# MLP products of an attention-and-MLP kernel: three float32r products of split operands in place of bilinear schemes, from the third unit on

## The chip, the cores and the metric

The kernel runs on one core of a Trainium2 chip. A core has five engines that matter here, each with a queue of its own that it works off in order: PE multiplies matrices, DVE and ACT work elementwise (ACT also evaluates functions), POOL is a slower elementwise engine, and SP issues DMAs. They wait for each other through semaphores. The metric is the device time of one execution in microseconds (us); the kernel before takes 545.12 us (median of three runs, 545.11 to 545.23).

## The reference

Two blocks follow each other. The first is a gated linear attention with a state per head, the second an MLP with an ELU between its two matrices:

```python
f = 1.0 / (1.0 + np.exp(-f_logit))                       # (4, 8, 768, 48)
for t in range(S):
    state = f[:, :, t, :, None] * state + np.einsum('bhd,bhe->bhde', k[:, :, t], v[:, :, t])
    y[:, :, t] = np.einsum('bhd,bhde->bhe', q[:, :, t], state)
x = y.transpose(0, 2, 1, 3).reshape(4 * 768, 8 * 48)     # 3072 tokens of 384
h = x @ w_in                                             # w_in (384, 2048), float64 on input
g = np.where(h > 0.0, h, np.exp(np.minimum(h, 0.0)) - 1.0)
out = g @ w_out                                          # w_out (2048, 384)
```

## The kernel before

The 3072 tokens are worked off as 12 units of 256 tokens, three to each of the four sequences. For a unit the attention is computed first, which leaves the unit's 256 rows of x, transposed (384 x 256), and then the MLP. The MLP of one unit and the attention of the next are interleaved: the program is written out in positions T, `plan` holds for each position the pieces of attention and other side work (`at_step`), and the main loop at the end of `fast` puts the MLP's matmuls between them. What is recorded in this order is each engine's queue order; no scheduler moves anything.

Attention of a unit, with the functions that do it: `load` fetches f, k, q and v; `gates` (ACT) and `grow` (a running product on DVE) make the decays, `fall` their reciprocals on DVE; `scale` multiplies them into k and q on POOL; `move` copies two of the decay rows' pieces to the fourth head pair with a DMA on SP's queue; `transposed` turns k on PE; `advance` makes the four chunks' state updates on PE and `step` adds them up on DVE; `scores` multiplies k and q on PE and `mask` cuts off the upper triangle on DVE; `outputs` and `carried` multiply by v and the state on PE, and ACT copies the result to x. Tiles of q, k and f are there twice, so that two units can be under way.

The weights come in as float64. `fetch`, `split`, `lower` and `merge` bring them in and make float32 of them during units 0 and 1; later `reread` and `check` read them again and look for values out of range, which is no part of the result but of a flag that chooses between this program and a general one.

In units 0 and 1 the up product (x by `w_in`) is plain: `up` takes two 128-column blocks of the hidden layer at a time, 3 x 2 matmuls of 256 columns. Unit 0's down product and two pairs of unit 1's are plain too (`down`, matmuls of 384 or 192 columns); the other pairs of unit 1 and all that follow use a 2 x 2 scheme with seven products for eight, whose sums of weights `combine` makes beforehand and whose sums of activations `elu` puts on POOL. From unit 2 on the up product uses a scheme with 20 products for 24: `phase` multiplies 128 x 128 blocks of weights, or sums of such (`w_sums`), by blocks of x or their sums (`blend`), and `joins` puts the results together on DVE, in the order that the tables `PHASES`, `JOIN3`, `MID`, `JOIN4` and `LAST` set. `exped` and `elu` are the ELU: two ACT operations and one DVE operation on 512 columns. All matmuls are float32. There are 20 positions T per unit from unit 2 on, and the tables `D2` to `D6`, `A2` and `A3` say at which of them attention's pieces stand: the third entry of `D5` and `D6`, -5, is that of the third decay and of `move`, the second entry of `A3`, 9, that of `advance` and `scores`.

Of the kernel before, what the change touches and what calls it, by code (L numbers as in the profile page):

```python
# [11 lines left out]
U16 = mybir.dt.uint16  # L12
AF = mybir.ActivationFunctionType
# [343 lines left out]
def fast(ctx: ExitStack, tc: tile.TileContext, q, k, v, f_logit, w_in, w_out, out, flag, outer):  # L357
# [7 lines left out]

# [26 lines left out]
    DH = DM // 2  # L392
    DIRECT = 1
    PLAIN_UP = 2
    NQ = NP // 2
    PLAIN = 2
    LAG = 2
    AHEAD = 7
# [4 lines left out]
    MORE = 3  # L403
    RR = 2
    HOLD = 2
    A1 = (2, 8, 10, 11)
    D2 = (16, 18, 20, 22)
    A2 = (23, 25, 25, 26, 27, 28)
    D3 = (-9, -6, -3, 1)
    D4 = (-9, -5, -1, 1)  # L410
    D5 = (-15, -9, -5, 1)
    D6 = (-19, -15, -5, 1)
    A3 = (3, 9, 12, 13)
    BL = 16
    BL2 = 29
    CB = 18
    LIMIT = 2.0**80

    X_SUMS = (
        ((12, 13), (1, 2), (0, 0)), ((10, 11), (2, 2), (3, 4)), ((9, 14), (1, 4), (5, 10)),  # L420
        ((8, 15), (0, 13), (9, 10)), ((1, 2), (3, 14), (1, 5)), ((6, 7), (4, 11), (8, 9)),
    )
    W_SUMS = (
# [4 lines left out]
    )  # L428
    EARLY = 10
    PHASES = (  # L430
# [5 lines left out]
    )  # L436
    SEED = (1, 3)
    JOIN3 = (
        (ALU.add, (4, 11), (4, 11), 1, (1, 2)), (ALU.add, (0, 12), (4, 9), 1, (0, 3)), (ALU.subtract, 4, 6, 1, 1, True),
    )  # L440
    MID = (ALU.add, (1, 5), (1, 5), None, (9, 11)), (ALU.subtract, (8, 9), (5, 5), None, (8, 12))
    JOIN4 = (ALU.add, (3, 6), (2, 11), 0, (0, 2)), (ALU.subtract, 2, 3, 0, 3)
    LAST = ((ALU.add, (3, 7), (3, 10), None, (4, 7)),)
    PLACES = ((0, ((0, 1), (1, 1), (1, 0), (0, 0))), (6, ((1, 0), (0, 0), (1, 1), (0, 1))))
    USUAL = ((0, 0), (0, 1), (1, 0), (1, 1))
# [7 lines left out]
    sb = ctx.enter_context(tc.tile_pool(name="sb", bufs=2))  # L453
    ps = ctx.enter_context(tc.tile_pool(name="ps", bufs=1, space=bass.MemoryType.PSUM))

    NB = 2

    qkf = [
        {n: cst.tile([128, HP, 2, U] if n == "f" else [128, HP, U], FP32, name=f"{n}{i}") for n in "fqk"}
        for i in range(NB)  # L460
    ]
    src = {"q": q, "k": k, "f": f_logit}
    vs = [cst.tile([128, NW, PAD + DM + PAD], FP32, name=f"v{i}") for i in range(NB)]
    kn = cst.tile([128, HP, NW, 128], FP32, name="kn")
    ats, xts, sts, pys = {}, {}, {}, {}

    def load(u, names="fkqv"):
        b, s0 = u // UPB, (u % UPB) * U
        for n in names.replace("v", ""):
            to = qkf[u % NB][n][MAIN]  # L470
            frm = src[n][b, :, :, s0 : s0 + U].rearrange("(p r) d s -> (r d) p s", r=2)
            if n == "f":
                to, frm = to[:, 0:NKT, 0], frm[:, 0:NKT]
            nc.sync.dma_start(out=to, in_=frm)
            for r in range(2 if n == "f" or n == "k" and u > 1 else 0):
                gap = qkf[u % NB][n][GAP[r] : GAP[r] + PAD, 0:NKT]
                nc.sync.dma_start(
                    out=gap[:, :, 0] if n == "f" else gap,
                    in_=src[n][b, 2 * NKT + r, :, s0 : s0 + U].rearrange("(i j) s -> i j s", i=PAD),
                )  # L480
# [912 lines left out]
```

## Time and profile before

| | |
|---|---|
| median of three runs | 545.12 us |
| span of the profiled execution | 544.3 us |
| instructions in it | 15606 |
| granted PE clock, mean | 0.998 |
| PE / DVE / ACT / POOL busy in the span | 528.5 / 407.5 / 314.5 / 338.4 us |
| units 0 and 1's MLP | 33.7 to 119.6 us |
| units 2 to 11's MLP | 119.6 to 539.1 us |

The profile names groups of instructions by line, engine, operation, output and inputs. "PE" rows are matmuls, "PEld" the loads of their weights. A float32 matmul leaves two records. Busy times are sums over the records of an engine, so that a share near 100% says that the engine hardly waited; "idle before" in a group's row is how long its engine stood still before these instructions, and what released it. The chain of waits is followed back from the last instruction: where a stretch of it belongs to PE, PE was what everything waited for.

### The profile page before, as it was taken

What the parts mean: (1) busy time and instruction counts of PE and PEld (TensorE: products, weight loads), DVE (VectorE), ACT (ScalarE), POOL (GpSimd) and SP (SyncE); (2) the same over time, 40 slices, a digit from 0 to 9 for tenths busy, and PEclk for the clock granted to TensorE, in tenths of its full rate; (3) what the DMA queues carried; (4) which work ended last, traced back from release to release, by engine and by line L of the source; (5) the groups of instructions that cost most, each with busy time, mean ns of one, the idle gap of its engine ahead of it and who ended that gap; (6) DMA issues with size and microseconds to landing.
All of it is one profiled execution on the core that took longest, in us unless ns stands there. A gap on an engine that the chain in (4) does not pass through costs nothing.

```text
span 544.3 us, 15606 instructions
## 1 busy us (share of the span) xinstructions
PE 528.5 (97%) x6294; PEld 492.8 (91%) x6294; DVE 407.5 (75%) x718; ACT 314.5 (58%) x644; POOL 338.4 (62%) x560
## 2 busy tenths in 40 slices
PE   6889999999999999999999999999999999999996
PEld 3477778899999999899999999999999999999995
DVE  8988988875978886687687687677777865644663
ACT  3289775136565567567567566566675565574441
POOL 6600337678898298298298288378478567454452
PEclk9999999999999999999999999999999999999999
DMA  8998971024052271271261252153243212110001
GB/s 211 256 272 233 282 191 47 2 51 104 30 126 80 57 200 30 61 202 32 61 183 52 60 148 86 60 140 94 60 133 102 61 29 83 50 50 1 29 3 36
DMA packets 39475, 54.30 MB, mean 100 GB/s; under 512 B 4032, under 2 KB 29216, under 8 KB 39392
## 3 DMA queue, kind: packets, MB, share of 16 engines
q1 hardware_dynamic: 38592, 52.61, 36.1%
q8 instruction: 51, 0.84, 0.7%
q10 hardware_dynamic: 800, 0.59, 0.4%
q14 instruction: 32, 0.26, 0.2%
HBM read 45.02 MB, written 4.72 MB: 91 GB/s over the span
## 4 chain that ended last, share of the span: by engine, by line
PE 89%; DMA 6%; DVE 2%; POOL 1%; issue 0%; ACT 0%; SPq 0%; ACTq 0%; DVEq 0%; POOLq 0%
PE psM L1063 37%; PE psH L965 33%; PE psH L989 6%; DMA area<-in_moe_w_in_dram 4%; PE psM L1025 3%; PE psY L804 2%; PE psY L828 2%; PE psU_a L789 2%; PE psS L766 2%; PE psT L726 1%; DMA f<-f 1%; DMA k<-in_k_dram 1%; DVE vals L955 1%; POOL k L678 0%; DVE gg L999 0%
## 5 line engine op out<-in xcount | busy, mean ns | idle before, releaser
L1012 POOL TENSOR_TENSOR sums<-gg 128x128 f32<-128x128 f32 x172 | 101.8, 611 | 124.1 <-DVE gg L999 119.1
L971 ACT COPY vals<-psH 128x512 f32<-128x512 f32 (+1 forms) x120 | 65.4, 545 | 122.2 <-PE psH L965 122.0
L965 PE MATMUL psH<-xt,wi 128*128 128x128 f32 x880 | 131.4, 276 | 0.1
L955 DVE TENSOR_TENSOR vals<-vals,psH 128x256 f32<-128x256 f32 (+1 forms) x160 | 61.8, 386 | 85.0 <-PE psH L965 46.3
L965 PE MATMUL psH<-xt,area 128*128 128x128 f32 x720 | 118.0, 277 | 0.5 <-DVE vals L955 0.4
L965 PEld LDWEIGHTS psH<-xt,wi 128*128 128x128 f32 x880 | 115.2, 192 | 0.7 <-DVE gg L999 0.3
L1063 PE MATMUL psM<-area,sums 128*128 128x192 f32 x516 | 103.3, 326 | 0.0
L965 PEld LDWEIGHTS psH<-xt,area 128*128 128x128 f32 x720 | 100.8, 191 | 2.0 <-PE psS L766 0.7
L1063 PEld LDWEIGHTS psM<-area,sums 128*128 128x128 f32 x516 | 85.9, 190 | 0.0
L1063 PE MATMUL psM<-wo,gg 128*128 128x192 f32 x376 | 76.7, 329 | 0.0
L999 DVE SCALAR_TENSOR_TENSOR gg<-gg,vals 128x512 f32<-128x512 f32 x80 | 64.1, 837 | 9.4 <-ACT gg L980 9.4
L955 DVE TENSOR_TENSOR vals<-vals 128x256 f32<-128x256 f32 x120 | 64.2, 549 | 2.0
L688 DVE RECIPROCAL f<-f 128x256 f32<-128x256 f32 x36 | 62.8, 1748 | 1.1
L1063 PEld LDWEIGHTS psM<-wo,gg 128*128 128x128 f32 x376 | 61.1, 190 | 1.8 <-DVE at L774 1.6
L980 ACT ACTIVATE gg<-gg 128x512 f32<-128x512 f32 x96 | 60.5, 631 | 3.1
L979 ACT ACTIVATE gg<-vals 128x512 f32<-128x512 f32 x80 | 49.5, 619 | 17.5 <-DVE vals L955 17.3
L678 POOL TENSOR_TENSOR k<-k,f 128x256 f32<-128x256 f32 x48 | 36.0, 752 | 32.0 <-DVE f L683 23.4
L678 POOL TENSOR_TENSOR q<-q,f 128x256 f32<-128x256 f32 x48 | 39.6, 826 | 18.8 <-DMA f<-f 14.6
L945 POOL TENSOR_TENSOR xt<-xt 128x256 f32<-128x256 f32 x57 | 48.6, 868 | 3.2 <-DVE xt L945 1.8
L1012 POOL TENSOR_TENSOR sums<-sums,gg 128x128 f32<-128x128 f32 x86 | 47.5, 552 | 0.2
L989 PE MATMUL psH<-xt,wi 128*128 128x256 f32 x192 | 44.8, 383 | 2.3 <-DVE xt L885 1.7
L1012 POOL TENSOR_TENSOR sums<-gg,sums 128x128 f32<-128x128 f32 x86 | 40.5, 471 | 6.6
(113 smaller groups left out, 741.8 us busy)
## 6 DMA issues: line engine op xcount, KB each, us to landing
area<-in_moe_w_out_dram SPq DMA_DIRECT2D x8, 768.0 KB, 10.6
again<-in_moe_w_in_dram SPq DMA_DIRECT2D x16, 384.0 KB, 4.5
again<-in_moe_w_out_dram SPq DMA_DIRECT2D x16, 384.0 KB, 3.6
k<-in_k_dram SPq DMA_DIRECT2D x12, 384.0 KB, 4.2
q<-in_q_dram SPq DMA_DIRECT2D x12, 384.0 KB, 5.4
v<-in_v_dram SPq DMA_DIRECT2D x12, 384.0 KB, 5.7
area<-in_moe_w_in_dram SPq DMA_DIRECT2D x8, 576.0 KB, 8.7
out_dram<-o SPq DMA_DIRECT2D x42, 96.0 KB, 1.7
```

The costliest lines, as they stand in the source:

```text
L678: e.tensor_tensor(out=t[n][:, p], in0=t[n][:, p], in1=t["f"][:, p, "kq".index(n)], op=ALU.mult)
L688: nc.vector.reciprocal(f[:, p, 1], f[:, p, 0])
L945: e.tensor_tensor(out=pick(x, to), in0=pick(x, a), in1=pick(x, b), op=ALU.subtract)
L955: nc.vector.tensor_tensor(out=pick(v, to), in0=x, in1=y, op=op)
L965: nc.tensor.matmul(bank[:, slot], lhsT=w_block(q, w), rhs=xts[m][:, x], start=(i < 2 and t == 0), stop=True, skip_group_check=True,)
L971: nc.scalar.copy(v[:, at : at + size], bank[:, frm : frm + size])
L979: nc.scalar.activation(g[:], h, AF.Relu, scale=-1.0)
L980: nc.scalar.activation(g[:], g[:], AF.Exp, scale=-1.0)
L989: nc.tensor.matmul(ph[:, i], lhsT=wi[j][:, kt, i * 128 : (i + 1) * 128], rhs=xts[m][:, 2 * kt : 2 * kt + 2].rearrange("n t f -> n (t f)"), ...
L999: nc.vector.scalar_tensor_tensor(out=g[:], in0=g[:], scalar=-1.0, in1=phs.pop(P), op0=ALU.add, op1=ALU.max)
L1012: nc.gpsimd.tensor_tensor(out=s[:, i], in0=x, in1=y, op=op)
L1063: nc.tensor.matmul(pm[bank][:, half * DH : (half + 1) * DH], lhsT=x, rhs=y, start=first, stop=(j == NP - 1), skip_group_check=True,)
```

## The change

The bilinear schemes, with their tables, weight sums and joins, are gone. Units 0 and 1 are plain in both products. From unit 2 on each float32 operand a is written as three float32r tiles of at most 12 significant bits (h, l and a sum or difference of them, scaled by powers of two), and a product of two float32 matrices is three matmuls that add up in two PSUM banks:

- `pieces` splits a weight item of 768 columns once: one ACT operation, one DVE operation, and a third part on DVE or on POOL (two operations there). Eleven of the 16 items are split during unit 1, five during unit 2. The parts lie where the float64 and float32 forms lay.
- `factor` splits x of a unit, `cut` the activations g, both through `parted`: ACT makes h, DVE l, POOL the difference. There is one tile of split x for all units, and two slots of split g.
- `top` does the up product of one 128-column block in nine matmuls of 256 columns, `joined` puts its two banks together (a copy on ACT, one operation on DVE), `curve` and `bent` are the ELU, `fold` does the down product in six matmuls of 384 columns, four positions (`BEHIND`) after `top`. `finish` puts the down product's two banks together at the end of a unit.

A unit has 16 positions now. f, k, q and v have one tile each from unit 2 on, so `attention(u)` runs from position -4 to 11 of the unit before. `check` takes 24 pieces of 512 columns in place of 32 of 384.

```diff
-    PHASES = (
-        (0, 1, 0, 3, ((1, 8, 16), (0, 9, 13), (2, 14, 12))),
...
+    E = 2.0**-12
+    CUT = 1.0 - 2.0**-13
...
+    def pieces(n, last):
+        tops[n] = sb.tile([128, 2, 2 * DM], F32R, tag=f"p{n}", name=f"top{n}")
+        h, l = tops[n][:, 0], tops[n][:, 1]
+        nc.scalar.activation(h, full[n][:], AF.Copy, scale=CUT / E)
+        nc.vector.scalar_tensor_tensor(
+            out=l, in0=full[n][:], scalar=1.0 / E, in1=h.bitcast(FP32), op0=ALU.mult, op1=ALU.subtract
+        )
+        rests[n] = sb.tile([128, 2 * DM], F32R, tag=f"r{n}", name=f"rest{n}")
+        d = rests[n][:]
+        if last is nc.vector:
...
+        nc.gpsimd.tensor_scalar(out=d, in0=h.bitcast(FP32), scalar1=-E, scalar2=None, op0=ALU.mult)
+        nc.gpsimd.tensor_tensor(out=d, in0=d.bitcast(FP32), in1=l.bitcast(FP32), op=ALU.add)
...
-    def attention(u, first, then):
+    def attention(u):
+        t = (u - 1) * NFT
...
+            at_step(t - 4, lambda: load(u))
+        at_step(t - 2, lambda: gates(u, bias=0))
...
+        at_step(t - 1, one, *(lambda p=p: (grow(u, p), scale(u, ("k", p, gp))) for p in range(2)))
+        at_step(t + 1, lambda: grow(u, 2), lambda: watch(u), lambda: scale(u, ("k", 2, gp)), lambda: move(u, 0, nc.sync))
+        at_step(t + 2, lambda: transposed(u, 0, "a0"), lambda: transposed(u, 1, "a1"))
+        at_step(t + 3, lambda: fall(u, 0), lambda: scale(u, ("k", NKT, gp), ("q", 0, gp)))
+        at_step(t + 4, lambda: advance(u))
+        at_step(t + 5, lambda: fall(u, 1), lambda: scale(u, ("q", 1, gp)))
+        at_step(t + 6, *(lambda c=c: step(u, c) for c in range(NC - 1)))
+        at_step(t + 7, lambda: fall(u, 2), lambda: scale(u, ("q", 2, gp)), lambda: move(u, 1, nc.sync))
+        at_step(t + 8, lambda: step(u, NC - 1), lambda: scale(u, ("q", NKT, gp)))
+        at_step(t + 9, lambda: kept.append(scores(u)), lambda: mask(u, kept[0]))
+        at_step(t + 10, lambda: outputs(u))
+        at_step(t + 11, lambda: carried(u))
...
+    def parted(x, to, halves):
+        h, l, d = to
+        nc.scalar.activation(h, x, AF.Copy, scale=CUT * E)
+        nc.vector.scalar_tensor_tensor(
+            out=l, in0=h.bitcast(FP32), scalar=-1.0 / E, in1=x, op0=ALU.mult, op1=ALU.add
+        )
...
+            nc.gpsimd.tensor_tensor(out=d[:, c], in0=h[:, c].bitcast(FP32), in1=l[:, c].bitcast(FP32), op=ALU.subtract)
...
+        for kt in kts:
+            for i in range(3):
+                nc.tensor.matmul(
+                    ph[:, i == 2], lhsT=ws[i][:, kt, s % 2 * 128 : s % 2 * 128 + 128], rhs=x[:, i, kt],
...
+    def joined(T):
...
+        nc.scalar.copy(to, ph[:, 1])
+        nc.vector.scalar_tensor_tensor(out=to, in0=ph[:, 0], scalar=1.0 + E, in1=to, op0=ALU.mult, op1=ALU.add)
...
+        for t in range(NW):
+            for n in range(3):
+                nc.tensor.matmul(
+                    pms[m][2 * t + (n == 2)][:], lhsT=g[:, P % 2, n, i * U + t * 128 : i * U + (t + 1) * 128],
+                    rhs=ws[n][:, i], start=(s == 0 and n != 1), stop=(s == NFT - 1), skip_group_check=True,
...
+    for T in range(begin, end + BEHIND):
+        u, s = divmod(T, NFT)
...
+            top(T)
...
+                bent(P - 1)
...
+            joined(T)
+        if T % 2 == 0 and begin < T <= end:
+            cut(P - 1)
+        if T % 2 and T < end:
+            curve(P)
         for f in plan.pop(T, ()):
             f()
...
+            fold(T - BEHIND)
```

On DVE in a unit in the middle, before: `vals` are the joins of the up product (L955), `gg` the ELU (L999), `f` the decays: a scan (L683) and a reciprocal (L688).

```order
L707 SCALAR_TENSOR_TENSOR fine<-f_71,fine 128x3
L683 SCALAR_TENSOR_TENSOR f_68<-f_68 128x256
L688 RECIPROCAL f_68<-f_68 128x256
L955 TENSOR_TENSOR vals_128<-vals_128,psH_0_1_3164 128x2x128 x2
L955 TENSOR_TENSOR vals_128<-psH_0_1_3164,vals_128 128x128
L999 SCALAR_TENSOR_TENSOR gg_6_3181<-gg_6_3181,vals_129 128x512
L999 SCALAR_TENSOR_TENSOR gg_7_3184<-gg_7_3184,vals_129 128x512
```

On DVE in the changed program, positions 7 to 9 of a unit: `v` is written by `joined` (L972), `g` with 128x512 by `bent` (L982) and by the split's subtraction (L943), `state` by `step`, `at` by `mask`, and L641 is `fall`.

```order
L972 SCALAR_TENSOR_TENSOR v_3742<-psH_3758,v_3742 128x256
L641 RECIPROCAL f_74<-f_74 128x256
L982 SCALAR_TENSOR_TENSOR g_3770<-g_3770,v_3742 128x512
L972 SCALAR_TENSOR_TENSOR v_3794<-psH_3783,v_3794 128x256
L943 SCALAR_TENSOR_TENSOR g_1260<-g_1260,g_3770 128x512
L691 TENSOR_TENSOR state<-psU_a_3661,state 128x4x48
L696 TENSOR_TENSOR state<-state,f_74 128x4x48
L972 SCALAR_TENSOR_TENSOR v_3794<-psH_3814,v_3794 128x256
L718 TENSOR_TENSOR at_3863<-psS_0_3829,twice 128x512
```

The reciprocal stood between joins of a program that had 20 positions per unit; it now stands between `joined` and `bent` of the running pair, and the state operation L696, which reads the decay row that `move` copies, stands ahead of the next `joined`.

On PE in the changed program, the same place: `psM` rows are `fold` (L1001), `psH` rows `top` (L960), and the first two of `scores`' 32 matmuls (L709) follow.

```order
L1001 MATMUL psM_0_3698<-top_1074,g_1260 128x384 x2
L1001 MATMUL psM_1_3699<-rest_1077,g_1260 128x384
L1001 MATMUL psM_2_3700<-top_1074,g_1260 128x384 x2
L1001 MATMUL psM_3_3701<-rest_1077,g_1260 128x384
L960 MATMUL psH_3814<-x_1173,top_1027 128x256 x2
L960 MATMUL psH_3814<-x_1173,rest_1030 128x256
L709 MATMUL psS_0_3829<-q_75,k_76 64x64
L709 MATMUL psS_1_3830<-q_75,k_76 64x64
```

Before, the scores stood directly behind the state updates `psU`; now five positions lie between them, and the scores stand two positions behind the last reciprocal.

More of the change, by code (lines that the diff above doesn't have):

```diff
@@ L12 @@
 U16 = mybir.dt.uint16
+F32R = mybir.dt.float32r
 AF = mybir.ActivationFunctionType
@@ L584, in fast, with shaped @@
-    order = [divmod(i, NP) for i in range(NU * NP)]
-    needs = sorted(
-        (2 * P + out_ * (2 * LAG + 1), j, out_) for P, (m, j) in enumerate(order) if m == 0 for out_ in range(2)
-    )
+    raws, full, tops, rests = {}, {}, {}, {}
+    needs = sorted((2 * j + out_ * (2 * LAG + 1), j, out_) for j in range(NP) for out_ in range(2))
     parts = [need[1:] for need in needs]
+    item = {part: n for n, part in enumerate(parts)}
+    def shaped(n, x):
+        return x.rearrange("p (k f) -> p k f", k=2 if parts[n][1] else NKT)
@@ new lines, in fast, with finish, store @@
+    left = []
+    def finish(m, sums):
+        o = outer.tile([128, NW, DM], FP32, tag="o", name=f"o{m}", bufs=1)
+        for t, (a, b) in enumerate(sums):
+            nc.scalar.copy(o[:, t], b[:])
+            if a is not None:
+                nc.vector.scalar_tensor_tensor(
+                    out=o[:, t], in0=a[:], scalar=1.0 + E, in1=o[:, t], op0=ALU.mult, op1=ALU.add
+                )
+        def store(*queues):
+            for t in range(NW):
+                queues[t].dma_start(out=out[m * U + t * 128 : m * U + (t + 1) * 128, :], in_=o[:, t])
+        if m == NU - 1:
+            left.append(store)
+        else:
+            store(nc.sync, nc.sync)
@@ new lines, in down @@
+    def down(P):
+        m, j = divmod(P, NP)
+        if j == 0:
+            banks = (("m1", "m2"), ("m3", "m0"))[m]
+            pms[m] = [ps.tile([128, DM], FP32, tag=banks[t], name=f"psM{m}_{t}") for t in range(NW)]
+        g = gs.pop(P)
+        for i in range(2):
+            for t in range(NW):
+                nc.tensor.matmul(
+                    pms[m][t][:], lhsT=g[:, i * U + t * 128 : i * U + (t + 1) * 128], rhs=weight(j, 1)[:, i],
+                    start=(j == 0 and i == 0), stop=(j == NP - 1 and i == 1),
+                )
+        if j == NP - 1:
+            finish(m, [(None, b) for b in pms.pop(m)])
@@ new lines, in parted, with top @@
+        n = x.shape[1] // halves
+        for i in range(halves):
+            c = slice(i * n, (i + 1) * n)
+            nc.gpsimd.tensor_tensor(out=d[:, c], in0=h[:, c].bitcast(FP32), in1=l[:, c].bitcast(FP32), op=ALU.subtract)
+    def top(T, kts=range(NKT)):
+        s = T % NFT
+        if T not in phs:
+            phs[T] = ps.tile([128, 2, U], FP32, tag=f"h{T % 2}", name=f"psH{T}")
+        ph, x = phs[T], exact["x"]
+        ws = three(s // 2, 0)
+        for kt in kts:
+            for i in range(3):
+                nc.tensor.matmul(
+                    ph[:, i == 2], lhsT=ws[i][:, kt, s % 2 * 128 : s % 2 * 128 + 128], rhs=x[:, i, kt],
+                    start=(kt == i == 0), stop=(kt == NKT - 1 and i > 0), skip_group_check=True,
+                )
@@ new lines, in bent, with cut, fold @@
+    def bent(P):
+        g = gs[P][:]
+        nc.vector.scalar_tensor_tensor(
+            out=g, in0=g, scalar=-1.0, in1=phs.pop(-P), op0=ALU.add, op1=ALU.max
+        )
+        del hs[P]
+    def cut(P):
+        if "g" not in exact:
+            exact["g"] = sb.tile([128, 2, 3, 2 * U], F32R, tag="wide", name="g3")
+        parted(gs.pop(P)[:], [exact["g"][:, P % 2, i] for i in range(3)], 2)
+    def fold(T):
+        m, s = divmod(T, NFT)
+        if s == 0:
+            pms[m] = [ps.tile([128, DM], FP32, tag=f"m{i}", name=f"psM{m}_{i}") for i in range(2 * NW)]
+        ws, g = three(s // 2, 1), exact["g"]
+        P, i = divmod(T, 2)
+        for t in range(NW):
+            for n in range(3):
+                nc.tensor.matmul(
+                    pms[m][2 * t + (n == 2)][:], lhsT=g[:, P % 2, n, i * U + t * 128 : i * U + (t + 1) * 128],
+                    rhs=ws[n][:, i], start=(s == 0 and n != 1), stop=(s == NFT - 1), skip_group_check=True,
+                )
+        if s == NFT - 1:
+            p = pms.pop(m)
+            finish(m, [(p[2 * t], p[2 * t + 1]) for t in range(NW)])
```

607 lines of the change are left out of this document (185 added, 422 removed), and 8 rows, old and new, of tables (PHASES, W_SUMS).

## The prediction

> **What bounds the kernel now.** I read the page's shares first, then the busy time by stage, then the chain that ended last.
>
> ```profile
> PE 528.5 (97%) x6294; PEld 492.8 (91%) x6294; DVE 407.5 (75%) x718; ACT 314.5 (58%) x644; POOL 338.4 (62%) x560
> ...
> 33.70:119.60 85.90, 85.09 (x884) 68.64 (x883) 72.51 (x106) 52.83 (x66) 37.85 (x52) 1.00 0.55 143
> 119.60:537.50 417.90, 417.01 (x5054) 407.84 (x5053) 303.79 (x570) 249.30 (x559) 281.82 (x464) 1.00 0.29 80
> ...
> 240.69 1.63 PE psM L1063 x10
> 282.38 1.63 PE psM L1063 x10
> ```
>
> The second row is units 0 and 1, the third units 2 to 11: PE is busy in 417.01 of 417.90 us, DVE in 303.79. The two chain rows are the same piece of work one unit apart, 41.7 us. So a unit costs what its matmuls cost, and everything on DVE, ACT and POOL is hidden. The prices of the matmuls are in the chain too, as stretches in which PE waits for nobody:
>
> ```profile
> 73.42 2.59 PE psH L989 x12
> 76.01 2.58 PE psM L1025 x8
> 254.94 2.23 PE psH L965 x20
> 257.17 2.28 PE psM L1063 x14
> ```
>
> A float32 product leaves two records. One record takes 215.8 ns at 256 columns (2.59/12), 322.5 at 384 (2.58/8), 111.5 at 128 (2.23/20) and 162.9 at 192 (2.28/14): time goes with the columns streamed.
>
> **The change on PE.** A step T (one 128-column block of the hidden layer) now has nine products of 256 columns (`top`) and six of 384 (`fold`). No row shows a float32r product. Upper bound: it costs one float32 record of its own width, 215.8 and 322.5 ns. Lower bound: a 12-bit part against a 12-bit part is one of the four part products of two 24-bit operands, so a quarter of two records, which is a record of half the width: 111.5 and 162.9. I take the lower bound, because the operands are cut to exactly that, and keep the upper as a rival. (The Trainium skill, FP8 and Floating Point Precision, TensorE Precision Notes, says that true FP32 takes four passes and that a reduced reading truncates a 4-byte operand; an estimate by it is 107.9 and 161.3 ns, and the time 7 us less. No run here shows such a product.) Then `top` is 9 x 111.5 = 1.00 us, `fold` 6 x 162.9 = 0.98, a step 1.98, 160 steps 316.9. Attention's matmuls stay; nine of them fall after the switch:
>
> ```profile
> 248.39 0.66 PE psT L726 x6
> 302.69 1.08 PE psU_a L789 x64
> 303.77 0.96 PE psS L766 x64
> 476.49 1.09 PE psY L804 x64
> 479.78 1.09 PE psY L828 x64
> 119.66 0.83 PE L965 MATMUL psH<-xt,area 128*128 128x128 f32 x6
> 538.29 0.81 PE L1063 MATMUL psM<-wo,sums 128*128 128x192 f32 x4
> 539.92 0.26 DVE o L1073
> ```
>
> They are 4.88 us a unit, 43.9 in all. The first quad starts at 119.66; unit 1's down products become plain, 2.58 for 2.28 four times, so 120.9. Two plain pairs of unit 1 still follow the switch, 5.2. Sum 120.9 + 316.9 + 43.9 + 5.2 = 486.9. At the end one pair's curve and split lie bare, 1.8 (priced below), two sums of 0.55 and a copy ahead of them 1.6, and from DVE's last sum at 540.2 to the span's end at 544.3 the store's 4.1. **The floor, PE never waiting, is 494.4**, a unit with attention 36.6 in place of 41.7.
>
> **What must keep up.** The other engines' prices:
>
> ```profile
> L999 DVE SCALAR_TENSOR_TENSOR gg<-gg,vals 128x512 f32<-128x512 f32 x80 | 64.1, 837 | 9.4 <-ACT gg L980 9.4
> L955 DVE TENSOR_TENSOR vals<-vals 128x256 f32<-128x256 f32 x120 | 64.2, 549 | 2.0
> L955 DVE TENSOR_TENSOR vals<-vals,psH 128x256 f32<-128x256 f32 x120 | 50.3, 419 | 83.6 <-PE psH L965 46.3 <-ACT vals L971 30.1 <-PE psT L726 3.8
> L688 DVE RECIPROCAL f<-f 128x256 f32<-128x256 f32 x36 | 62.8, 1748 | 1.1
> L683 DVE TENSOR_TENSOR_SCAN f<-f 128x256 f32<-128x256 f32 x36 | 28.9, 810 | 1.9 <-ACT f L671 1.9
> L774 DVE TENSOR_TENSOR at<-psS,twice 128x512 f32<-128x512 f32 x24 | 15.4, 684 | 1.8 <-POOL area L1206 1.1 <-PE psS L766 0.6
> L747 DVE TENSOR_TENSOR state<-psU_a,state 128x192 f32<-128x192 f32 x40 | 14.2, 355 | 2.3 <-PE psU_a L789 1.1
> L1073 DVE TENSOR_TENSOR o<-psM,u 128x384 f32<-128x384 f32 x10 | 5.5, 547 | 0.0
> L1182 DVE TENSOR_SCALAR f<-f 128x768 f32<-128x768 f32 x1 | 0.6, 631 | 0.0
> L707 DVE SCALAR_TENSOR_TENSOR fine<-f,fine 128x3 f32<-128x3 f32 x12 | 4.3, 359 | 0.0
> L752 DVE TENSOR_TENSOR state<-state,f 128x192 f32<-128x192 f32 x8 | 3.2, 400 | 0.3
> L980 ACT ACTIVATE gg<-gg 128x512 f32<-128x512 f32 x96 | 60.5, 631 | 3.1
> L979 ACT ACTIVATE gg<-vals 128x512 f32<-128x512 f32 x80 | 49.5, 619 | 17.5 <-DVE vals L955 17.3
> L730 ACT COPY kn<-psT 128x256 f32<-128x256 f32 x14 | 5.5, 390 | 7.9 <-PE psT L726 6.7 <-DVE f L688 1.2
> L678 POOL TENSOR_TENSOR k<-k,f 128x256 f32<-128x256 f32 x48 | 36.0, 752 | 32.0 <-DVE f L683 23.4 <-DMA f<-f 6.2 <-PE psY L804 1.6
> ```
>
> Removed are the sums of the bilinear schemes (L955, L1012, L945, L930, L580). Added on DVE per pair of steps: two `joined` at 0.42, `bent` and the split's subtraction at 0.84: 2.51 us. Eight pairs are 20.1. Attention and the unit's ends add three reciprocals 5.24, three scans 2.43, one add 0.63, five state sums 1.82, two masks 1.37, the watch 0.36, two output sums 1.09 and three splits of x 1.65: 14.6. **DVE has 34.7 us of work in a unit whose PE floor is 36.6**, 95%, where it had 303.79 of 417.90. On an in-order queue at that load the order decides. The three places where I see PE wait are worked out with 0.08 us per hand-over:
>
> ```profile
> 532.08 0.63 ACT L980 ACTIVATE gg<-gg 128x512 f32<-128x512 f32 x1
> ...
> 532.79 0.69 DVE L999 SCALAR_TENSOR_TENSOR gg<-gg,vals 128x512 f32<-128x512 f32 x1 [1.47 <-ACT gg L980]
> ...
> f<-f SPq DMA_DIRECT2D x20, 96.0 KB, 4.9
> ...
> xt<-xt SPq DMA_DIRECT2D x20, 48.0 KB, 2.2
> ```
>
> (a) Transposes at step 2. After `top` of step 1: copy 0.39, `joined` 0.42, scan 0.81, POOL's k 0.75, four hand-overs 0.32, 2.69 us; PE has a fold, a top and four of six transposes, 2.42. Wait 0.3.
>
> (b) The fold of step 4 reuses the banks that `finish` reads. On DVE `finish` stands behind a reciprocal: after `top` of step 3 copy 0.39, `joined` 0.42, reciprocal 1.75, two sums 1.09, hand-overs 0.24, 3.9 us; PE has a fold, a top and psU, 3.06. Wait 0.8.
>
> (c) The scores at step 9 need the last reciprocal of step 7, moved by a DMA, then multiplied on POOL: copy 0.39, `joined` 0.42, reciprocal 1.75, move, POOL's q at k's 0.75, hand-overs 0.40, 3.71 plus the move. The change moves 48 KB at a time. Like rows are 2.2 us (as many bytes, another tile) and 4.9 (the same tile, twice the bytes); I take 3.5 for both ends being equally near, so 7.2. PE has two folds and two tops, 3.96. Wait 3.3, bounds 2.0 and 4.7. In the old order the move is issued at position -5 and the scores come at 9, of 20 positions per unit, 29 us by the 41.7; now it is two steps, 3.96.
>
> (d) DVE is late when it gets to that reciprocal. From step 14 of the unit before to step 7 it owes, pair by pair, 6.41, 3.68, 5.35, 4.26 and 5.33: 25.0 us. PE does 5 x 3.96 + 0.66 + 1.08 = 21.5, and waits 1.1 in (a) and (b). So the reciprocal is 2.4 late, and what it holds up with it (the state sum that waits for the same move stands ahead of the next `joined`). After step 9 PE has attention's long products and DVE catches up, so it repeats each unit but does not grow.
>
> Together 6.8 a unit, bounds 3.1 (c low, no lag) and 8.2; nine units have attention behind them: 61. ACT and POOL have no wait of their own here, but their queues pass DVE's lateness on, which I don't add. The bare end of 1.8: copy 0.39, `joined` 0.42, 0.62, 0.63, 0.84, split 0.62, 0.84, POOL 0.75, hand-overs 0.64, 5.75, against four folds, 3.9.
>
> (e) Five weight splits fall into steps 0 to 8 of unit 2, each with two POOL operations of 768 columns. At k's 2.9 ns a column one is at most 2.3 us, so up to 23 us beside some 12 that POOL owes there anyway, in some 22 us. Bounds 0 and 10, I take 4. In unit 1 the eleven earlier ones lie beside a PE busy 85.09 of 85.90 and cost nothing if POOL's k and q don't queue behind them; if they do, one split, some 4 us.
>
> Sum: 494.4 + 61 + 4 = 559.4 for this execution, whose span is 544.3; the median of the runs is 545.1, 0.8 above it. **Forecast 560 us, slower by 2.7%.** Break-even is (545.1 - 494.4 - 0.8)/9 = 5.5 us of waiting a unit.
>
> **Rivals.** *A, the queues keep up* (faster). For it: the old kernel hid 73% of DVE, and L955's 419 against 549 shows that means hold waits that can shrink. Against it: 95%. With (a), (b), (c low) and no lag, 3.1 a unit: 494.4 + 28 + 0.8 = 523; without any wait 495. It wins below 5.5 a unit.
>
> *B, a float32r product costs a whole record.* A step is 9 x 215.8 + 6 x 322.5 = 3.88 us, 160 steps 304 us more than above, everything else hidden: about 799. Against it stands only the argument from the widths.
>
> *C, the clock falls in the wait for the scores.* The granted clock here is 1.00 while PE works:
>
> ```profile
> 538.00:540.00 2.00, 1.11 (x7) 0.81 (x5) 1.83 (x5) 0.00 (x0) 0.00 (x0) 1.00 0.21 62
> 540.00:542.00 2.00, 0.00 (x0) 0.00 (x0) 0.18 (x1) 0.00 (x0) 0.00 (x0) 1.00 0.51 153
> 542.00:544.30 2.30, 0.00 (x0) 0.00 (x0) 0.00 (x0) 0.00 (x0) 0.00 (x0) 0.54 0.06 16
> ```
>
> PE's last matmul ended at 539.1, and a mean of 0.54 over 2.3 us is half clock from 542.2 on: 3.1 us of idleness were enough. A wait of 3.3 to 5.7 reaches that. If the array then needs as long, 3.1 us, to come back, each unit loses 1.6, nine 14: 574; twice as long 588. For it: (c). Against it: (c low) is under 3.1. (The Trainium skill, TensorE: Matmul & The Clock Gate, Part 1, states this gate, with free-running windows of about 3.4 us in both directions; an estimate by it is 1.7 a unit. The trace agrees as far as the 3.1 us go.)
>
> **How the numbers follow.** The waits as summed 0.50, own range 547 to 600; C 0.10; B 0.05; A 0.31; within 0.2% (what a measurement here can tell from no change) 0.04, the waits happening to be 5.5. Faster: A and a hundredth of the first, 0.32; slower 0.64. The range from 505 to 605 leaves out B, A's best tenths and the upper tail of C.
>
> **What would show it.** In the changed profile: PE records of 256 columns 107 to 112 ns apart (else B); DVE at 80 to 85% of the span, PE near 80%; PE idle ahead of psS, released by POOL's q or its DMA, as the longest wait (c), ahead of psM by DVE o (b), ahead of psT by POOL k (a); units of 43 to 45 us; the granted clock below 1.00 inside units (C). Wrong would be a PE over 95% busy in units 2 to 10, or DVE's added operations well under 0.84 and 0.42.

## The result and the profile after

The changed kernel takes 647.7 us (median of 4 runs, 644.5 to 650.7), the kernel before 545.2 in the same comparison: 1.185 times as long, with a 95% interval of 1.180 to 1.191. The forecast was 560, the range 505 to 605. The direction was right, the size was not: 103 us in place of 15. The profiled execution has a span of 648.9 us.

First the page of the changed kernel: busy time, the slices of the granted clock, and the shares of the chain that ended last.

```profile
PE 561.4 (87%) x5916; PEld 499.0 (77%) x5916; DVE 410.0 (63%) x636; ACT 358.2 (55%) x739; POOL 296.4 (46%) x348
...
PEclk9999998979798898988979979889899979879997
...
PE 27%; DVE 23%; ACT 20%; POOL 11%; issue 8%; DMA 7%; SPq 1%; ACTq 0%; POOLq 0%; DVEq 0%
```

Before, PE was busy 97% and the clock full. Now less than a third of the chain is PE, DVE, ACT and POOL together are over half, and none of them is near full. So no engine's amount of work alone sets the time; what sets it is work handed from one queue to the next. And the granted clock is below 0.9 in 17 of the 40 slices.

Next the span cut by stages (up to the first float32r product, unit 2, units 3 to 10, unit 11 with the end). The columns are the length, the busy time of PE, PEld, DVE, ACT and POOL, the granted clock, the DMA share and GB/s.

```profile
0.00:134.10 134.10, 116.47 (x1187) 80.51 (x1188) 96.11 (x131) 73.03 (x97) 50.53 (x66) 0.96 0.62 152
134.10:192.60 58.50, 46.97 (x480) 42.13 (x479) 36.98 (x54) 27.39 (x59) 44.86 (x39) 0.88 0.12 29
192.60:598.30 405.70, 358.22 (x3986) 338.40 (x3985) 253.79 (x409) 233.58 (x538) 184.47 (x224) 0.92 0.27 77
598.30:648.90 50.60, 39.78 (x267) 37.97 (x266) 23.13 (x45) 24.20 (x47) 16.54 (x22) 0.93 0.05 18
```

Set against the terms of the prediction, these four stages add up as follows. The forecast for unit 2 is the floor of 36.6, waits of 6.8, 4 for weight splits and 5.2 for the plain products left over; the last one is what remains of 559.4.

```
stage                              forecast   measured   difference
up to the first float32r product    120.9      134.1       +13.2
unit 2                               52.6       58.5        +5.9
units 3 to 10, eight                347.2      405.7       +58.5   (43.4 and 50.7 a unit)
unit 11 and the end                  38.7       50.6       +11.9
sum                                 559.4      648.9       +89.5
```

Then what a float32r product costs, from the chain of waits of the changed kernel. Each row is a stretch in which PE works through one block: the start, the length, the tile and the number of records.

```profile
602.40 1.04 PE psM L1001 x6
603.44 1.07 PE psH L960 x9
...
328.57 1.92 PE psH L960 x9
```

A float32r product leaves one record, where a float32 product left two. At full clock it takes 119 ns at 256 columns (1.07/9) and 173 at 384 (1.04/6), so a step is 2.11 us. The last row is the same block inside a stretch at half clock (324.8 to 331.6 us): 1.92 us.

Last, the long waits of PE and PEld in the whole span (total, times, longest):

```profile
PEld psT L670 <- POOL k L632: 25.8, 13, 2.7
PEld psS L709 <- POOL q L632: 23.6, 14, 3.3
...
PEld psM L1001 <- POOL g L949: 9.3, 13, 3.3
...
PE psS L709 <- DVE state L691: 8.7, 5, 1.9
...
PEld psH L960 <- POOL x L949: 7.9, 11, 3.6
```

PE waits for POOL at two places of each unit: ahead of the transposes, for k's scaling, and ahead of the scores, for q's.

The waits are best seen step by step. This table is worked out from the trace's records: the time from the first up product of a step to that of the next, in unit 5, one of the middle ones. 2.1 is a step without any wait. Attention's own matmuls belong to steps 2 (0.7), 4 (1.1), 9 (1.0), 10 and 11 (1.1 each); steps 14 and 15 are interleaved and stand together.

```
step             0   1   2   3   4   5   6   7   8   9  10  11  12  13  14  15   sum
own work       2.1 2.1 2.8 2.1 3.2 2.1 2.1 2.1 2.1 3.1 3.2 3.2 2.1 2.1   4.2    38.7
after          3.2 2.2 6.2 3.0 3.5 2.1 2.1 2.1 2.1 7.7 4.8 3.4 2.1 2.1   4.6    51.3
after, unit 11 2.9 2.1 2.1 2.1 3.5 2.1 2.1 2.1 2.1 2.1 2.1 2.1 2.1 2.1
```

In the last row no unit's attention runs beside the MLP any more, and a step takes 2.1 us, PE's own pace, in all but steps 0 and 4. So, those two steps aside, the MLP by itself is hidden, splits and all. The time is lost where attention's chain and the MLP's share the queues: steps 2 and 3, 9 and 10.

### The profile page after: what moved, and what is told of

It is laid out like the page before. It is cut to its first block, busy times and chain, and to the rows that moved or that the text cites. A ratio compares the mean times of both kernels' runs of the same rounds, so it can differ in the third digit from the quotient of the medians.

```text
span 648.9 us, 14650 instructions
## 1 busy us (share of the span) xinstructions
PE 561.4 (87%) x5916; PEld 499.0 (77%) x5916; DVE 410.0 (63%) x636; ACT 358.2 (55%) x739; POOL 296.4 (46%) x348
## 4 chain that ended last, share of the span: by engine, by line
PE 27%; DVE 23%; ACT 20%; POOL 11%; issue 8%; DMA 7%; SPq 1%; ACTq 0%; POOLq 0%; DVEq 0%
PE psH L960 10%; PE psM L1001 10%; POOL g L949 4%; ACT g L942 4%; DVE g L982 4%; DVE g L943 4%; DVE v L972 3%; ACT g L977 3%; DVE f L637 3%; ACT v L971 3%; ACT g L978 2%; DMA f<-in_f_logit_dram 2%; POOL k L632 2%; PE psY L748 2%; ACT again L616 2%
## 5 line engine op out<-in xcount | busy, mean ns | idle before, releaser
L949 POOL TENSOR_TENSOR g<-g 128x256 fp32r<-128x256 f32 x160 | 124.2, 797 | 182.9 <-DVE g L943 115.3
L960 PE MATMUL psH<-x,top 128*128 128x256 f32 x960 | 191.9, 296 | 0.8
L1001 PE MATMUL psM<-top,g 128*128 128x384 f32 x640 | 177.0, 359 | 1.2 <-ACT v L971 1.1
L960 PEld LDWEIGHTS psH<-x,top 128*128 128x128 f32 x960 | 166.6, 202 | 5.4 <-DVE v L972 4.7
L960 PE MATMUL psH<-x,rest 128*128 128x256 f32 x480 | 142.1, 296 | 5.6 <-POOL x L949 5.5
L972 DVE SCALAR_TENSOR_TENSOR v<-psH,v 128x256 f32<-128x256 f32 x160 | 66.7, 418 | 109.4 <-ACT v L971 109.4
L1001 PE MATMUL psM<-rest,g 128*128 128x384 f32 x320 | 114.0, 356 | 5.6 <-POOL g L949 5.6
L1001 PEld LDWEIGHTS psM<-top,g 128*128 128x128 f32 x640 | 114.2, 199 | 4.7 <-DVE o L903 1.3
L960 PEld LDWEIGHTS psH<-x,rest 128*128 128x128 f32 x480 | 96.9, 202 | 7.9 <-POOL x L949 7.9
L942 ACT ACTIVATE g<-g 128x512 fp32r<-128x512 f32 x80 | 50.7, 633 | 56.5 <-DVE g L982 56.5
L982 DVE SCALAR_TENSOR_TENSOR g<-g,v 128x512 f32<-128x512 f32 x80 | 58.7, 734 | 32.9 <-ACT g L978 32.9
L943 DVE SCALAR_TENSOR_TENSOR g<-g,g 128x512 fp32r<-128x512 f32 x80 | 58.4, 730 | 23.9 <-ACT g L942 21.6
L1001 PEld LDWEIGHTS psM<-rest,g 128*128 128x128 f32 x320 | 63.7, 199 | 9.3 <-POOL g L949 9.3
L641 DVE RECIPROCAL f<-f 128x256 f32<-128x256 f32 x30 | 52.2, 1742 | 0.0
L924 PE MATMUL psM<-full,g 128*128 128x384 f32 x128 | 47.7, 519 | 0.5 <-DVE full L568 0.5
```

The lines of the kernel that those rows point to most:

```text
L942: nc.scalar.activation(h, x, AF.Copy, scale=CUT * E)
L943: nc.vector.scalar_tensor_tensor(out=l, in0=h.bitcast(FP32), scalar=-1.0 / E, in1=x, op0=ALU.mult, op1=ALU.add)
L949: nc.gpsimd.tensor_tensor(out=d[:, c], in0=h[:, c].bitcast(FP32), in1=l[:, c].bitcast(FP32), op=ALU.subtract)
L960: nc.tensor.matmul(ph[:, i == 2], lhsT=ws[i][:, kt, s % 2 * 128 : s % 2 * 128 + 128], rhs=x[:, i, kt], start=(kt == i == 0), stop=(kt == N ...
L972: nc.vector.scalar_tensor_tensor(out=to, in0=ph[:, 0], scalar=1.0 + E, in1=to, op0=ALU.mult, op1=ALU.add)
L982: nc.vector.scalar_tensor_tensor(out=g, in0=g, scalar=-1.0, in1=phs.pop(-P), op0=ALU.add, op1=ALU.max)
```

## The experiments

All compare with the changed kernel at 647.7 us, whose own runs differ by 1%; the experiments were one execution each, so differences under some 6 us are not read. The kernel before took 545.4 to 549.7 beside them. Where a unit's time is given without more, it is the mean of units 3 to 10 (50.7 in the changed kernel).

**1. Dummy products in PE's two long waits.**

```
-  at_step(t + 2, lambda: transposed(u, 0, "a0"), ...)
+  at_step(t + 2, lambda: warm(3, "h1") if u > 2 else None, lambda: transposed(u, 0, "a0"), ...)
-  at_step(t + 9, lambda: kept.append(scores(u)), ...)
+  at_step(t + 9, lambda: warm(4, "h0") if u > 2 else None, lambda: kept.append(scores(u)), ...)
```

> From unit 3 on, three dummy products of 512 columns stand ahead of the transposes and four ahead of the scores, where PE waits longest; nothing else differs. Half-clock theory: the granted clock falls only because PE idles there, and the products that run at half speed cost about 2.5 us a unit (17.4 us in the seven units from 199.3 to 553.8); the clock's mean rises from 0.93 to 0.98 or more and the time falls to about 626. Queue theory: PE's products then only arrive earlier at the same late operands, the half clock lay beside the waits, and the time stays above 638. If the dummies are longer than the waits they cost up to 1 us a unit, 9 us.

635.5 us. The stretch of units 3 to 10 of this kernel:

```profile
193.60:583.00 389.40, 378.43 (x4098) 331.87 (x4096) 253.81 (x409) 234.84 (x538) 184.53 (x225) 1.00 0.28 80
```

The clock is 1.00 there, where it was 0.92, and a unit takes 48.7: the edit gains 2.0 us a unit, and the whole got shorter by 12. That is between the two expectations: steps 3 and 10 fall to 2.1 and 3.4, about their own work, and step 2 to 5.8, but most of the waiting is still there. What stays with the clock held, 48.7 less 38.7, is 10.0 us a unit: 3.0 at step 2, 4.6 at step 9, 1.1 at step 0, 0.3 at step 4, the rest in small pieces. Some of this is the dummies' own time. By the traces, the transposes end 0.74 us after POOL's k here and 0.49 in the changed kernel where the clock holds, the scores 1.36 to 1.48 after POOL's last q here and 0.52 there. By these distances, as an estimate, some 1.1 us a unit of the 10.0 can be the dummies', so that the half clock costs between 2.0 and 3.1 us a unit and the waits come to between 8.9 and 10.0.

**2. The reciprocals made cheap.**

```
-  nc.vector.reciprocal(of(u)["r"][:, p], of(u)["f"][:, p])
+  nc.vector.tensor_scalar(out=of(u)["r"][:, p], in0=of(u)["f"][:, p], scalar1=2.0**-100, ..., op0=ALU.mult)   # from unit 2 on
```

> From unit 2 on each reciprocal is a multiplication by a constant of the same 256 columns (the output is then not the reference's). Theory of the late DVE: the three cost about 0.3 us each in place of 1.74, 4.3 us less on DVE in a unit, the wait for the scores (3.7 us a unit) falls below 1, and the time to about 605. Rival, the waits come from POOL's and ACT's queues or from the DMA move: the time stays above 630 and PE still waits over 2.5 us ahead of the scores.

640.2 us, little against the 40 expected of DVE's lateness. DVE's busy time falls by 34 us and the waits ahead of the transposes (26.1 us of PEld) and of the scores (21.2) stay as they were. What holds q now is seen in POOL's and DVE's rows around one unit's scores (start, length, operation, count, and in brackets the idle time before):

```profile
317.73 1.53 POOL L954 TENSOR_TENSOR g<-g 128x256 fp32r<-128x256 f32 x2 [2.14 <-DVE g L948]
319.23 0.72 POOL L632 TENSOR_TENSOR q<-q,f 128x256 f32<-128x256 f32 x1
...
317.89 0.79 DVE L701 TENSOR_TENSOR state<-state,f 128x192 f32<-128x192 f32 x1
```

DVE's product for the carried state needs the same DMA move as q and begins at 317.89, so the move has landed by then; q's scaling begins at 319.23 only because POOL's two subtractions for g's third part stand ahead of it, and these waited 2.14 us for DVE's split.

**3. No third part of g.**

```
-  nc.gpsimd.tensor_tensor(out=d[:, c], in0=h..., in1=l..., op=ALU.subtract)      # for g as for x
+  if halves == 1: nc.gpsimd.tensor_tensor(...)                                    # for x alone
-  lhsT=g[:, P % 2, n, ...]
+  lhsT=g[:, P % 2, min(n, 1), ...]
```

> POOL does not make the third part of g (two subtractions a pair, 1.6 us of POOL, 12.8 us a unit); the third product reads the second part instead, so the output is not the reference's. Theory that k's scaling on POOL waits in line behind those subtractions, and that they slow DVE while they run: the wait for the transposes (2.5 us a unit) falls below 0.5, DVE's split and curve operations get shorter than 0.73 us, and the time falls to about 615. Theory that DVE alone is late: POOL's scaling still waits for DVE's scans and reciprocals, and the time stays above 635.

605.1 us, 43 less; a unit takes 45.6. Step 2 falls from 6.2 to 3.9, step 0 from 3.2 to 2.6, step 9 to between 6.0 and 6.4 in five of the eight units. POOL's q and DVE's scans in this kernel, and the scans in the changed one, by groups (count, busy us, mean ns, and idle time before with its releasers):

```profile
L632 POOL TENSOR_TENSOR q<-q,f 128x256 f32<-128x256 f32 x40 | 38.3, 959 | 109.6 <-DVE f L641 93.6 <-DMA f<-f 16.0
L637 DVE TENSOR_TENSOR_SCAN f<-f 128x256 f32<-128x256 f32 x33 | 24.2, 762 | 1.3 <-ACT f L625 1.0
```

```profile
L637 DVE TENSOR_TENSOR_SCAN f<-f 128x256 f32<-128x256 f32 x33 | 35.4, 1099 | 1.6 <-ACT f L625 1.2
```

So two things end with POOL's subtractions: k and q no longer queue behind them, and DVE's scans, which read two tensors from SBUF, take 762 ns in place of 1099. (The Trainium skill, SBUF — State Buffer, SBUF: two separate sides, says that DVE with two SBUF inputs and GpSimd take turns on a shared pair of ports, an exclusive lock; these two rows agree with it.) The expectation that split and curve would get shorter was wrong: they take 750 and 722 ns, for 730 and 734. Ahead of the scores q now waits for the reciprocal and for the move's DMA.

**4. PE's part of attention one step later.**

```
-  at_step(t + 2, transposed ...) ... at_step(t + 9, scores ...) ... at_step(t + 11, carried)
+  at_step(t + 3, transposed ...) ... at_step(t + 10, scores ...) ... at_step(t + 12, carried)
```

> PE's part of attention (transposes, state products, scores, outputs) comes one step later in each unit, and what DVE and POOL do before it stays where it is. Theory that the waits are distances too short by two to four us: both long waits shrink by up to a step, 2.1 us each, 9 units: about 612. Theory that the engines are simply full: the lateness comes out at the next place (the split of x and the first products of the next unit) and the time stays above 638.

627.6 us, a unit 47.7: between the two expectations. Nothing is lost at the transposes any more (0.7 stays at step 2, where the down products wait for g's third part), some 2 us a unit ahead of the scores, and a new wait of over 2 stands at step 4, where the down products now come without other work ahead of them (PEld waits 18.7 us in all for DVE's output sums), with about 1 at step 11, where the outputs wait for the mask.

**5. g's third part behind k's and q's scalings on POOL.**

```
   (in parted, for g) thirds.append(third)              # in place of issuing it
   (in the loop, after the attention work of a step)
+  while T % 2 and thirds:
+      thirds.pop(0)()
```

> POOL's two subtractions for the third part of g are issued after the attention work of the following odd step, so that k's and q's scalings no longer stand behind them; every operation is kept. Theory of the order on POOL's queue: the step with the transposes falls from 6.3 us to about 4 and the one with the scores from 8 to about 6.3, as when the subtractions were left out; units of 45 to 46 in place of 50.6, time about 605 to 612. Rival, POOL's subtractions cost because they run beside DVE and slow it (or because POOL is simply full): the order gains nothing, the time stays above 635.

663.9 us, 16 more, against a gain of 40 expected. Waits of PE and PEld in this kernel:

```profile
PEld psM L1012 <- POOL g L953: 84.1, 43, 4.7
...
PEld psT L670 <- POOL k L632: 4.7, 5, 1.8
```

The wait ahead of the transposes is gone (25.8 to 4.7), and the one of the down products for g's third part has grown from 9.3 to 84.1, since POOL now stands waiting for DVE's scan or reciprocal with the subtractions behind it. The theory was right that the order on POOL makes the waits and wrong that the order has a free end. The time came out where the rival had it, above 635, but not for the rival's reason: DVE's scans take 748 ns on average here, as short as in run 3, POOL is busy 46% of the span, and the time rose all the same.

**6. No third parts of the weights on POOL.**

```
-  nc.gpsimd.tensor_scalar(out=d, in0=h..., scalar1=-E, ...)
-  nc.gpsimd.tensor_tensor(out=d, in0=d..., in1=l..., op=ALU.add)
...
+  ... rests[n][:] if n in rests else tops[n][:, 1] ...
```

> POOL makes no third parts of the weights (eleven times two operations of 768 columns, 47 us of POOL in units 1 and 2); the second part is read in their place. Theory that these put k and q of units 1 and 2 off: the wait of 3 us at unit 1's scores and the half clock after it go, the first float32r product comes at about 125 in place of 134, unit 2 takes about 50 in place of 58.5, time about 632. Rival, units 1 and 2 are late for the other reasons: the time changes by under 5 us.

637.3 us. The first float32r product comes at 129.4 in place of 134.1, and unit 2 takes 48.0 in place of 58.5; the units after it are as they were (50.9). Of the changed kernel, PE's rows in unit 1, where the first of the two losses before 134 stands too:

```profile
78.43 4.54 PE L879 MATMUL psH<-xt,full 128*128 128x256 f32 x12 [3.63 <-DVE g L894]
...
110.29 0.71 PE L709 MATMUL psS<-q,k 64*64 64x64 f32 x16 [3.06 <-POOL q L632]
110.93 5.49 PE L924 MATMUL psM<-full,g 128*128 128x384 f32 x8
...
121.41 2.85 PE L924 MATMUL psM<-full,g 128*128 128x384 f32 x8
```

The wait of 3.06 us for POOL's q goes with POOL's weight splits (0.17 is left), and with it the half clock that made the eight products behind it 5.49 us long where the same eight take 2.85 elsewhere. The first float32r product comes at 128.0 to 129.4 in the three runs that make no such third parts on POOL (6, 8 and 13) and at 130.1 to 135.6 in all others, so the gain is real and its size uncertain by some us. The wait of 3.63 us stays (3.49 here); DVE had stood still until 74.6 for a weight's DMA, as the chain of waits has it:

```profile
67.62 7.00 DMA raw<-in_moe_w_out_dram
...
74.64 0.57 DVE full L552
```

**7. and 8. The order of 5 with the later step of 4; then everything together.** The eighth makes all weight thirds on DVE and adds two dummy products ahead of transposes and scores.

> The subtractions of g's third part late on POOL, as in the first kernel of this call, and PE's part of attention a step later, as in an earlier run. If the two take away different waits their gains add: 20 us for the later step and some 40 for the order, about 590. If they are one and the same wait, the time is that of the better one, about 607 to 612.

> The order and the later step of the kernel before, with all third parts of the weights made on DVE (1.33 us for 4.28 on POOL) and two dummy products of 512 columns ahead of the transposes and of the scores from unit 3 on. If every wait named so far is what made the time, units come to 42 to 43 and the whole to about 565; if something else holds PE once these are gone, units stay at 44 or more and the time above 580.

692.4 us for 7, far outside both its expectations, and 696.7 for 8, so something else does hold PE. Edits 4 and 5 do not add, they harm each other: units of 55.7, since with PE's attention a step later the down products still wait for g behind q (85.8 us of PEld), steps 0 and 8 above all. The dummies and the weight thirds on DVE change little in that: units of 57.2.

**9. to 11. k and q scaled on DVE.** 9 moves only that; 10 adds the later step, 11 moreover puts the addition of one on ACT and the last reciprocal ahead of the state sums.

```
-  scale(u, ("k", p, gp))   scale(u, ("q", 1, gp)) ...
+  scale(u, ("k", p, dv))   scale(u, ("q", 1, dv), ("k", NKT, dv)) ...       # dv = nc.vector
-  at_step(t - 2, lambda: gates(u, bias=0)) ... at_step(t - 1, one, ...)      # 11 only
+  at_step(t - 2, lambda: gates(u)) ... at_step(t - 1, ...)
```

> From unit 2 on k and q are multiplied on DVE right behind the scan or reciprocal that they need, 8 operations of 256 columns a unit; POOL keeps only the third parts. Nothing is left out; k's last pair comes at step 5. Theory of the shared POOL queue (two streams that PE waits for stand in one line, in whichever order): DVE has some 3.5 us more to do in a unit and the unit still gets shorter, 45 to 46 us, time about 605. Theory that DVE's load of 95% is what makes PE wait (the one of the prediction): a unit gets longer by up to those 3.5 us, time 650 to 680.

> The same, with PE's part of attention, the state sums and q's last pair a step later. Shared-queue theory: what is left before the scores is the chain from the last reciprocal over its DMA move, about as long as the steps in between plus 2 us; a step more hides it, units of 42 to 43, time about 580. DVE theory: as the kernel before it, within 10 us.

> As the kernel before, with the addition of one to the gates on ACT (0.85 us) in place of DVE (1.05 us), and the last reciprocal ahead of the state sums on DVE. Shared-queue theory: DVE has room, so both matter by under 1 us a unit, within 10 us of the kernel before. DVE theory: DVE's shorter line shows in PE's waits at the transposes and the scores, 1.5 to 2 us a unit, 15 us or more.

646.7, 632.0 and 623.4 us. In 9 DVE has 37 us more to do and the time is the same as the changed kernel's. Neither theory fits alone: by DVE's load a unit gets longer by up to 3.5 us (it takes 50.3 for 50.7, though the whole is only 3 us short of the 650 expected), by the shared POOL queue the time is 605. A gain and a loss nearly cancel: step 2 falls from 6.2 to 4.8, step 9 rises from 7.7 to 8.1 in unit 5 (7.5 to 8.6 in the others):

```profile
PE 556.4 (86%) x5916; PEld 490.5 (76%) x5916; DVE 447.4 (69%) x716; ACT 357.9 (55%) x739; POOL 222.0 (34%) x268
```

```profile
PE psS L709 <- DVE state L691: 16.6, 6, 3.7
...
PE psS L709 <- DVE q L632: 13.2, 8, 3.4
```

The scores now wait for DVE's state sum (they are written to the PSUM banks that this sum reads) and for its q, and both stand in DVE's line with the split and the curve. 10 came to neither of its expectations. It ends 4 us above run 4, and 11, 8.5 below 10, ends 4 us below it: the later step does what it did there, and DVE's shorter line little beside it.

**12. Reciprocals and third part of g both out**, the edits of 2 and 3.

> Reciprocals as multiplications by a constant and no third part of g on POOL, both edits of earlier runs in one kernel (not the reference's output). Alone they gave 8 and 43 us, and each alone left the step with the scores at 6.0 to 6.5 us where the clock held. Theory of two chains side by side: with both out that step falls to about 5 (the DMA move is left) and the time by more than the sum of the two, to about 580 or below. Theory of one chain, on POOL: the reciprocals give their 8 us or less once more, the step stays at 6 and the time at 597 or above.

584.0 us, 64 less, where the two gave 8 and 43 alone. A unit takes 43.3, and step 9 falls to between 4.7 and 5.2. The time lies nearer the expectation of two chains (580) than that of one (597), and the step came out as the two chains have it. The excess over the sum, 13 us, is not far above the scatter of single executions; the rows of 2 and 3, in which the scores wait for one chain and then for the other, carry the conclusion more than the excess does. In units 3 to 10 alone a unit is 1.0 us shorter in 2, 5.1 in 3 and 7.4 here.

**13. All suspected causes out:** 12 with the later step, the addition of one on ACT and no POOL work for the weights.

> Both of these, PE's part of attention a step later, the addition of one on ACT, and no third parts of the weights on POOL (not the reference's output). If the waits that have been named are all there are, PE is left with its float32r products at the pace of the last unit (2.14 us a step) and attention's 4.9: units of 40 to 41, first float32r product at about 125, time about 540. If units stay above 43, there is a wait that was not named.

583.1 us, units of 44.5, so there was a wait that had not been named as one. Two rows of this kernel:

```profile
PEld psM L1003 <- DVE o L902: 16.0, 9, 2.5
...
PEld psY L751 <- DVE at L721: 8.8, 18, 0.9
```

With the transposes a step later, the first down products of a unit stand in the open behind the output sums (place (b) of the prediction), and the outputs right behind the mask. The later step, worth 20 us in 4, is worth nothing here, and the start and unit 2 win what units 3 to 10 lose.

**14. Only the up products as float32r.**

```
-  for n in range(3): nc.tensor.matmul(pms[m][2 * t + (n == 2)][:], lhsT=g[:, P % 2, n, ...], rhs=ws[n][:, i], ...)
+  nc.tensor.matmul(pms[m][2 * t][:], lhsT=gs[P][:, ...], rhs=weight(s // 2, 1)[:, i], ...)
-  cut(P - 1)
```

> Only the up products are made as three float32r products; the down products are plain float32 ones, four of 384 columns a step, 1.29 us for 1.06, so a PE floor of 42.8 us a unit in place of 39.1. The split of g (0.63 us of ACT, 0.73 of DVE, 1.6 of POOL a pair) and eight weight splits are gone. Theory that the chain of curve, split and third part in line with attention's scalings makes the time: units of 45 to 46, faster than the whole change by 40 us or more, about 600. Theory that joining the two up sums (ACT copy and DVE sum a step) makes it: the waits stay, units of 52 or more, time 655 or more.

593.0 us, 55 less than the whole change, with more PE work. The stretch from 193 to 533 us and the waits of this kernel:

```profile
193.00:533.00 340.00, 333.05 (x3608) 261.17 (x3601) 175.66 (x309) 195.72 (x451) 75.83 (x88) 1.00 0.31 87
```

```profile
PEld psS L709 <- POOL q L632: 11.5, 11, 2.1
...
PEld psT L670 <- POOL k L632: 4.8, 3, 3.3
```

PE is busy 333 of 340 us and the clock is full; a unit takes 44.7 against a floor of 42.8. The ACT copy and the DVE sum of every up step are still there and hold up little. So g's split costs most: it puts three more hand-overs (ACT, DVE, POOL) between the curve and the down products and lies on all the queues that attention needs. How much it costs alone is not shown, since this edit also makes PE's step longer (2.4 us for 2.1), which leaves every chain more time, and 11 of the 55 us are unit 2's (47.6 us), where leaving out weight splits alone won 10.5 in run 6. No version here beats the kernel before, whose unit took 41.7: the floor of this one is above that, and the whole change, with a floor of 38.7, has room for 3.0 us of waiting a unit (less what the start costs), where its best versions that leave nothing out, runs 4 and 11, have 9.0 and 9.2.

## Why the prediction was right in its direction and wrong in its size

**What bounds the kernel before, and that PE would wait for the other engines:** right. PE's share fell from 97% to 87%, and the places named, transposes, scores, first down products, are where it waits.

**The price of a product:** the lower bound, taken as the value, was too low by 6 to 7%: 119 and 173 ns measured for 111.5 and 162.9. A step is 2.11 for 1.98, 21 us over 160 steps, 2.1 a unit. The floor of a unit is 38.7, not 36.6. Rival B, a whole record, is out.

**DVE at 95%:** wrong as a number and, by itself, as a cause. In units 3 to 10 DVE is busy 253.8 us of 405.7, 31.7 a unit for 34.7 expected. The sum for the curve and the one for the split take 734 and 730 ns, not 840, and the scans took 1099, not 810. These prices depend on what POOL does meanwhile: in the kernel before, the curve's sum takes 682 ns on average where no POOL operation runs beside it and 892 where POOL works for at least three tenths of its time. And 34 us less on DVE gave 8 (run 2), 37 us more, with 74 less on POOL, gave none (run 9).

**The waits:** with the clock held (run 1) they are 8.9 to 10.0 us a unit for 6.8 forecast. (a), the transposes, was the term that was mis-sized: 2.7 to 3.0 for 0.3. DVE's lag was counted once, at the reciprocal (d); at the transposes it comes through ACT and POOL. The sentence that ACT's and POOL's queues pass DVE's lateness on, "which I don't add", is the step that failed. The changed kernel's rows ahead of unit 5's transposes show it; `top` of step 1 ended at 298.50:

```profile
299.22 0.63 ACT L942 ACTIVATE g<-g 128x512 fp32r<-128x512 f32 x1 [2.96 <-DVE g L982]
299.75 0.36 ACT L971 COPY v<-psH 128x256 f32<-128x256 f32 x1
...
300.83 1.17 DVE L637 TENSOR_TENSOR_SCAN f<-f 128x256 f32<-128x256 f32 x1
...
300.72 1.79 POOL L949 TENSOR_TENSOR g<-g 128x256 fp32r<-128x256 f32 x2 [1.00 <-DVE g L943]
302.48 1.24 POOL L632 TENSOR_TENSOR k<-k,f 128x256 f32<-128x256 f32 x1
```

k is ready at 303.72, 5.2 us after `top`, for the 2.7 worked out. ACT's copy starts 1.25 us after `top` because g's split stands ahead of it on ACT and had waited 2.96 us for DVE's curve. The scan, beside POOL, takes 1.17 for 0.81. Then k's scaling stands behind g's third part, which ends 0.5 after the scan, and takes 1.24 for 0.75.

(c) with (d), the scores, came to between 3.7 and 4.6 for 5.7; the wait was there, but not from the one chain worked out. Beside reciprocal, move and q runs a second chain, curve, split and third part, into the same POOL queue, and either alone holds PE about as long. (b) is 0.3 for 0.8 where attention runs, and 1.4 in unit 11 (3.5 less 2.1). A wait at step 0 was not on the list: 1.1 for the third parts of x and g on POOL, of which 0.6 went with g's in run 3.

**Rival C, the clock:** it happened, in each of units 2 to 10, along with the waits rather than in place of them. Up to PE's last product the trace's record of the clock holds 18 stretches at half, each of 3.41 or 6.83 us, 89 us in all, and run 1 prices them at 2.0 to 3.1 us a unit for the 1.6 estimated. (The Trainium skill, TensorE: Matmul & The Clock Gate, Part 1, has free-running windows of about 3.4 us; the stretches of one and of two such windows agree.) A chance of 0.10 was too low: the forecast's own waits of 5.7 at the scores were already above the 3.1 that the profile had shown to be enough.

**The start:** the weight splits of unit 1 were put at nothing "if POOL's k and q don't queue behind them", at some 4 us if they do. They do: 4.7 us (run 6). Another wait, of 3.63 us for a weight's DMA, with half-speed products behind it, was not seen at all. In unit 2 the splits cost 10.5 us for the 4 taken, just above the upper bound of 10.

**The end** took 8.0 us from DVE's last sum at 640.9 to the span's end where 4.1 were taken over from the kernel before. In the trace the last store, on ACT's queue, is only issued from 643.28 to 646.07, 2.79 us, where the kernel before issued two there in 1.17; why is open.

In units 3 to 10, then, the 7.3 us a unit that were missing are 2.1 of price, 2.0 to 3.1 of clock and 3.2 to 2.1 of waits. No one of them reaches the result alone.

## What to carry to other kernels

A change that moves work off the bounding engine is to be judged by its longest hand-over chain, not by the sums of busy time: here no other engine was above 63%, and PE still lost 12 us a unit. Where two chains for which the bounding engine waits pass through one in-order queue, follow both through that queue step by step; swapping their order only swaps who waits, and taking one away uncovers the other. And count the half clock behind a long wait as well. In the traces of the changed kernel and its fourteen variants, from 35 us to the last up product, PE came to stand still for 3.25 us or more 61 times while the clock was full, and each time a stretch at half clock began during that wait or within 3.5 us after it; for waits of 2.25 to 3.25 us it was 70 of 93, for 1.5 to 2.25 us 22 of 56.

## What was not expected of the hardware

A float32r product leaves one record and takes 119 ns for 256 columns and 173 for 384, that is 0.42 ns a column and some 11 ns besides; a float32 product left two records of 215.8 and 322.5. DVE's scan of 256 columns takes 678 to 693 ns where no POOL operation runs beside it, in the changed kernel (3 of 33 scans) as in run 3 (19 of 33), and 1140 on average in the 30 scans of the changed kernel beside which POOL works for at least three tenths of their time. The reciprocal (1734 to 1744 ns) and `joined` (407 to 426), which read at most one tensor from SBUF, show no such difference. And a wait of 3.06 us, before which PE had worked at full rate, was followed by half clock, eight products taking 5.49 us for 2.85.
